# Linear attention and a bilinear feed-forward on one core: the out stage of three groups as seven block products, and v by casting transfers

## Chip, cores, metric

One core of a Trainium2 chip. The metric is device time in microseconds of one execution, from three runs; the profile is of one more execution of the same program.

## What is computed

Attention with decay in blocks, for batch 4, 8 heads, 768 positions and head size 64, and behind it a feed-forward whose two hidden halves are multiplied with each other:

```
for b in range(nb):                       # blocks of 64 positions
    intra = einsum('bhij,bhjd->bhid', einsum('bhic,bhjc->bhij', qb, kb) * Dmask, vb)
    inter = einsum('bhid,bhde->bhie', qb * lam_pow, kv_state)
    out[:, :, sl] = intra + inter
    kv_state = lam_block * kv_state + einsum('bhsd,bhse->bhde', kb * rev_pow, vb)
x = out.transpose(0, 2, 1, 3).reshape(3072, 512)
a, b = x @ w_a, x @ w_b                   # 512 -> 1536
return (a * b) @ w_out                    # 1536 -> 512, float32
```

## The kernel before

A *unit* is a block of 128 positions of one batch entry with all 8 heads: 24 units, 6 to a batch entry. The units go through the feed-forward in eight groups of 4, 1, 2, 4, 4, 4, 4 and 1 units (`GROUPS`). All matmuls are bf16, all accumulation is in the eight banks of PSUM.

**A unit's attention.** SP loads q, k and v of the unit (L154, 256 KB each in runs of 256 bytes) into staging tiles, `pump` keeping two or three units ahead. `make_ks` and `make_qs` scale k and q with powers of lambda and cast them (L318, on GpSimd from unit 6 on), `make_vb` casts v (L337 or L335, on GpSimd, VectorE or ScalarE by `VB_ENG`). From unit 7 on a DMA transpose on SP turns q and k (L346); units 4 to 6 are transposed on TensorE (L360). `piece_S` makes the scores on TensorE (L374) and masks them from PSUM on VectorE (L391); `piece_V` adds the unit to the running state (L438) and copies it (L471 on VectorE, L469 on ScalarE); `pieces_O` computes the attention of one or two units (L408), and ScalarE copies it, transposed, into the group's x tile `xT` (L431).

**A group's feed-forward.** Groups 0, 1, 2 and 7 run `ffn`: for each of 12 blocks of 128 hidden columns an a product, a ScalarE copy (L519), a b product and a VectorE multiplication into `ab` (L510, L537); then the out products, 12 matmuls of 512 columns for each unit (L557), a copy (L552 or, in the first two groups, L548) and a store. Groups 3 to 6 (`Z_GROUPS`) run `ffn_z`, in which a and b are each made by a seven-product scheme for 2 x 2 blocks: six *pairs* (index n), each of seven products of four matmuls of 256 columns (L641, `product`), three copies of partial sums on ScalarE (L647, `snap`), three subtractions on VectorE (L679, L688, L689), and `finish`: the seventh product, a ScalarE copy (L656) and the VectorE multiplication into `ab` (L658). The sums of the weights (`weight_sum`, L212 to L218) and of xT (`x_sums`, L620 to L622) that the scheme needs are VectorE's. Then comes the out stage, 48 matmuls of 512 columns for a group (L697, `out_part`), in whose midst the last pair is finished.

**What sets the order.** The program is emitted by hand: each engine executes its instructions in the order in which they are emitted, waiting on semaphores. `PLAN` lists for every group at which slot (`hook(slot)`, called between the steps of `ffn` and `ffn_z`) which piece is emitted: C casts a part of w_out, PK, PV and P prepare a unit (k and q, v, all), T transposes, S, V and O or O2 are the pieces above, Q is an O2 with two score pieces, WS is a weight sum, X the sums of xT, W stores a row that was kept back. A piece that stands at a slot only fixes the place in each engine's queue; an engine that has its inputs runs ahead of TensorE.

Of the kernel before, what the change touches and what calls it, by code (L numbers as in the profile page):

```python
# [22 lines left out]
def _bc(ap, dims):  # L23
# [8 lines left out]
W_BUFS = 8  # L32
# [10 lines left out]
PLAN = {  # L43
    0: [(0, 'V', 3), (8, 'C', 0), (9, 'C', 1), (15, 'C', 2), (18, 'C', 3), (23, 'PK', 4),
        (26, 'C', 4), (26, 'T', 4), (27, 'WS', 0), (28, 'WS', 1), (29, 'C', 5), (29, 'S', 4),
        (30, 'PV', 4), (31, 'WS', 2), (32, 'WS', 3), (33, 'O', 4), (34, 'WS', 4),
        (35, 'PK', 5), (35, 'PV', 5)],
    1: [(0, 'V', 4), (2, 'T', 5), (3, 'PK', 6), (4, 'WS', 5), (6, 'PV', 6), (6, 'S', 5),
        (7, 'T', 6), (8, 'WS', 6), (10, 'S', 6), (11, 'WS', 7), (12, 'O2', (5, 6)),
        (13, 'P', 7)],  # L50
    2: [(2, 'V', 6), (2, 'P', 8), (3, 'P', 9), (4, 'W', None), (5, 'V', 7), (5, 'PK', 10),
        (7, 'V', 8), (8, 'S', 7), (8, 'S', 8), (10, 'V', 9), (10, 'W', None), (11, 'PV', 10),
        (11, 'W', None), (12, 'P', 11), (12, 'W', None), (12, 'Q', (7, 8, 9, 10)),
        (13, 'P', 12), (14, 'O2', (9, 10)), (15, 'X', 3), (15, 'P', 13), (15, 'W', None)],
    3: [(0, 'S', 11), (2, 'P', 14), (4, 'S', 12), (7, 'S', 13), (7, 'P', 15),
        (9, 'O2', (11, 12)), (11, 'S', 14), (11, 'V', 13), (15, 'P', 16),
        (16, 'O2', (13, 14)), (16, 'X', 4), (17, 'P', 17), (17, 'P', 18), (17, 'S', 15),
        (19, 'S', 16), (19, 'P', 19)],
    4: [(3, 'V', 11), (3, 'V', 15), (4, 'S', 17), (5, 'O2', (15, 16)), (6, 'S', 18),
        (7, 'P', 20), (8, 'O2', (17, 18)), (9, 'V', 17), (9, 'P', 21), (11, 'S', 19),  # L60
        (13, 'S', 20), (14, 'X', 5), (19, 'V', 19), (19, 'P', 22)],
    5: [(4, 'S', 22), (5, 'S', 21), (8, 'O2', (19, 20)), (10, 'V', 21), (11, 'O2', (21, 22)),
        (11, 'P', 23), (16, 'X', 6)],
    6: [(0, 'S', 23), (11, 'O', 23)],
}
Z_GROUPS = (3, 4, 5, 6)
KV_ENG = dict(enumerate(["dve"] * 10 +
                        ["act"] * 2 +
                        ["dve"] +
                        ["act"] * 3 +  # L70
                        ["dve"] * 6 +
                        ["act"] +
                        ["dve"]))
VB_ENG = dict(enumerate(["pool"] * 7 +
                        ["dve"] * 3 +
                        ["act"] * 2 +
                        ["dve"] +
                        ["pool"] * 4 +
                        ["dve"] +
                        ["pool"] * 2 +  # L80
                        ["act"] +
                        ["dve"] +
                        ["pool"] * 2))
# [3 lines left out]
def kernel(  # L87
# [25 lines left out]
    wst_pool = ctx.enter_context(tc.tile_pool(name="wst", bufs=W_BUFS))  # L113
    ld_pool = ctx.enter_context(tc.tile_pool(name="ld", bufs=4))
    prep_pool = ctx.enter_context(tc.tile_pool(name="prep", bufs=6))
# [3 lines left out]
    a_pool = ctx.enter_context(tc.tile_pool(name="a", bufs=4))  # L119
# [5 lines left out]
    sum_pool = ctx.enter_context(tc.tile_pool(name="sum", bufs=1))  # L125
    ctx.enter_context(tc.manual_schedule())
# [24 lines left out]
    def load_x(w, u):  # L151
        b, nb = divmod(u, NB)
        t = ld_pool.tile([128, H, D], F32, name=w + "f", tag=w + "f")
        nc.sync.dma_start(out=t, in_={"q": qr, "k": kr, "v": vr}[w][b, nb])  # L154
        raw[u, w] = t
# [7 lines left out]
    staged = {}  # L163
    w_off = [sum(W_CHUNKS[:i]) for i in range(len(W_CHUNKS) + 1)]
# [7 lines left out]
    def load_w(kind, c):  # L172
        t = wst_pool.tile([128, 1024], F32, name="wst", tag="wst")
        if kind == "o":
            t = t[:].rearrange("p (k n) -> p k n", k=2)
# [8 lines left out]
        staged[kind, c] = t  # L184

    def cast_w(kind, c, eng):
        t = staged.pop((kind, c))
# [4 lines left out]
        if eng == "act":  # L192
            nc.scalar.copy(dst, t)
        elif eng == "first":
# [3 lines left out]
        else:  # L198
# [4 lines left out]
    wz = {kind: sum_pool.tile([128, 4, 2, HF], BF16, name="wz_" + kind, tag="wz_" + kind)  # L203
          for kind in "ab"}

    def weight_sum(i):
        kind, j = "ab"[i % 2], i // 2
        w, z = (wa_sb if kind == "a" else wb_sb), wz[kind]
        a11, a12 = w[:, 0:2, :HF], w[:, 2:4, :HF]
        a21, a22 = w[:, 0:2, HF:], w[:, 2:4, HF:]  # L210
        if j == 0:
            nc.vector.tensor_sub(z[:, 0], a22, a21)  # L212
        elif j == 1:
            nc.vector.tensor_sub(z[:, 1], a11, z[:, 0])
        elif j == 2:
            nc.vector.tensor_sub(z[:, 2], a12, z[:, 1])
        else:
            nc.vector.tensor_add(z[:, 3], a11, a21)  # L218
# [6 lines left out]
    pending += [("o", 4), ("o", 5), ("v", n0)]  # L225
    for u in range(n0 + 1, NU):
        pending += [("q", u), ("k", u), ("v", u)]
    used = {"u": 0}

    def pump():  # L230
        while pending:
            kind, c = pending[0]
            if kind in "abo":
                if len(staged) >= W_BUFS:
                    return
# [8 lines left out]
    idle_sb = singles.tile([128, 512], BF16, name="idle_sb")  # L244
# [11 lines left out]

# [368 lines left out]
    def ffn_z(g, u0, xT, hook):  # L625
# [42 lines left out]
        for n in range(NP):  # L668
            if n != 1:
                begin(n)  # L670
# [253 lines left out]
```

## Time and profile before

| | |
|---|---|
| median of three runs | 228.94 us (227.91, 228.94, 229.74) |
| profiled execution | 228.72 us |
| its span, first to last instruction | 227.0 us, TensorE clock granted 1.00 |
| q, k or v of a unit, issue to landing, median | 5.0 to 5.4 us |
| DMA transpose of a unit, issue to landing | 4.8 us |
| a stored 256 KB, issue to landing | 2.2 us |

Busy time counts the time in which an engine executes; for TensorE it is that of matmuls, which overlap, so rates are read from starts that follow each other. A row of the groups gives line, engine, operation, what it writes and reads, count, busy time and mean duration, then the idle time ahead of it and what ended that. The chain of waits goes back from the last instruction to what released each step. "SPq" is SP's own queue, in which a DMA is issued.

### The profile page before, as it was taken

What the parts mean: (1) busy time and instruction counts of PE and PEld (TensorE: products, weight loads), DVE (VectorE), ACT (ScalarE), POOL (GpSimd) and SP (SyncE); (2) the same over time, 40 slices, a digit from 0 to 9 for tenths busy, and PEclk for the clock granted to TensorE, in tenths of its full rate; (3) what the DMA queues carried; (4) which work ended last, traced back from release to release, by engine and by line L of the source; (5) the groups of instructions that cost most, each with busy time, mean ns of one, the idle gap of its engine ahead of it and who ended that gap; (6) DMA issues with size and microseconds to landing.
All of it is one profiled execution on the core that took longest, in us unless ns stands there. A gap on an engine that the chain in (4) does not pass through costs nothing.

```text
span 227.0 us, 5349 instructions
## 1 busy us (share of the span) xinstructions
PE 217.8 (96%) x2127; PEld 148.3 (65%) x2127; DVE 154.6 (68%) x257; ACT 117.0 (52%) x233; POOL 59.2 (26%) x73
## 2 busy tenths in 40 slices
PE   7798999999899999999999999999999999999994
PEld 2374444447678758877458887448887458885493
DVE  0994773969959868999356988676988318773050
ACT  2685465037443267656247685127576236672261
POOL 6061000147843254424424434460000000000000
PEclk9999999999999999999999999999999999999999
DMA  4999999999999999999999999943020030000311
GB/s 131 318 261 350 359 387 319 271 222 196 233 192 200 240 187 269 212 233 184 181 247 237 205 186 231 169 153 92 3 48 1 27 144 18 1 3 0 141 46 46
DMA packets 97544, 39.40 MB, mean 174 GB/s; under 512 B 85488, under 2 KB 92016, under 8 KB 97520
## 3 DMA queue, kind: packets, MB, share of 16 engines
q1 hardware_dynamic: 97232, 39.00, 80.4%
q8 instruction: 16, 0.26, 0.5%
q10 hardware_dynamic: 288, 0.07, 0.1%
q14 instruction: 8, 0.07, 0.1%
HBM read 28.32 MB, written 6.29 MB: 152 GB/s over the span
## 4 chain that ended last, share of the span: by engine, by line
PE 77%; DMA 8%; SPq 6%; DVE 4%; issue 2%; ACT 1%; ACTq 0%; DVEq 0%
PE op L697 18%; PE U L641 15%; PE b_ps L510 9%; PE op L557 9%; PE a_ps L510 7%; PE V L641 7%; PE o_ps L408 4%; DMA wst<-in_moe_w_b_dram 4%; PE W L641 4%; SPq L154 3%; DMA qkT<-qk 3%; PE kq L374 2%; DMA q<-in_q_dram 2%; PE kvd L438 1%; SPq L183 1%
## 5 line engine op out<-in xcount | busy, mean ns | idle before, releaser
L697 PE MATMUL op<-wo_sb,ab 128*128 128x512 bf16 x192 | 43.3, 379 | 0.0
L391 DVE TENSOR_TENSOR m<-kq,lotri 128x512 bf16<-128x512 f32 x47 | 29.7, 681 | 13.7 <-PE kq L374 13.6
L647 ACT COPY u<-U 128x512 f32<-128x512 f32 x48 | 27.8, 587 | 18.7 <-PE U L641 17.9
L318 POOL TENSOR_TENSOR qk<-kf,lp_k 128x512 bf16<-128x512 f32 x18 | 19.7, 1096 | 53.2 <-DMA kf<-in_k_dram 51.0
L537 DVE TENSOR_TENSOR ab<-a_sb,b_ps 128x128 bf16<-128x128 bf16 (+2 forms) x48 | 19.3, 415 | 20.9 <-ACT a_sb L519 13.6
L697 PEld LDWEIGHTS <-ab 128*128 128x128 bf16 x192 | 18.2, 98 | 20.7
L318 POOL TENSOR_TENSOR qk<-qf,lp_q 128x512 bf16<-128x512 f32 x20 | 24.8, 1239 | 23.0 <-DMA qf<-in_q_dram 23.0
L510 PE MATMUL b_ps<-xT,wb_sb 128*128 128x128 bf16 (+2 forms) x192 | 27.6, 272 | 1.2 <-DVE wb_sb L199 1.0
L510 PE MATMUL a_ps<-xT,wa_sb 128*128 128x128 bf16 (+2 forms) x200 | 27.7, 268 | 0.0
L552 ACT COPY o_sb<-op 128x512 f32<-128x512 f32 (+2 forms) x21 | 11.1, 547 | 31.3 <-PE op L697 28.8
L658 DVE TENSOR_TENSOR ab<-oab 128x1024 bf16<-128x1024 bf16 x24 | 18.8, 783 | 9.1 <-ACT oab L656 9.0
L519 ACT CAST a_sb<-a_ps 128x128 bf16<-128x128 f32 (+2 forms) x48 | 17.2, 376 | 13.1 <-PE a_ps L510 11.5
L557 PE MATMUL op<-wo_sb,ab 128*128 128x512 bf16 (+2 forms) x120 | 22.5, 337 | 0.2 <-DVE ab L537 0.2
L510 PEld LDWEIGHTS <-wb_sb 128*128 128x128 bf16 x192 | 15.8, 98 | 7.7 <-DVE wb_sb L199 1.5
L641 PEld LDWEIGHTS <-wz_a 128*128 128x128 bf16 x192 | 18.3, 98 | 3.3 <-issue 0.3
L510 PEld LDWEIGHTS <-wa_sb 128*128 128x128 bf16 x200 | 16.0, 98 | 6.7 <-DVE wa_sb L199 0.4
L641 PEld LDWEIGHTS <-wz_b 128*128 128x128 bf16 x192 | 18.7, 97 | 2.2
L688 DVE TENSOR_TENSOR oab<-U,v 128x512 bf16<-128x512 f32 x24 | 16.4, 683 | 3.4 <-PE U L641 2.6
L641 PE MATMUL U<-xT,wz_a 128*128 128x256 bf16 x96 | 18.3, 272 | 0.0
L641 PE MATMUL U<-xT,wz_b 128*128 128x256 bf16 x96 | 18.3, 272 | 0.0
L679 DVE TENSOR_TENSOR oab<-W,u 128x512 bf16<-128x512 f32 x24 | 16.3, 681 | 0.9 <-PE W L641 0.9
L431 ACT CAST xT<-o_ps 128x512 bf16<-128x512 f32 (+1 forms) x24 | 12.2, 556 | 9.0 <-PE o_ps L408 8.9
(96 smaller groups left out, 337.0 us busy)
## 6 DMA issues: line engine op xcount, KB each, us to landing
vf<-in_v_dram SPq DMA_DIRECT2D x24, 256.0 KB, 5.0
qf<-in_q_dram SPq DMA_DIRECT2D x20, 256.0 KB, 5.1
kf<-in_k_dram SPq DMA_DIRECT2D x20, 256.0 KB, 5.4
out_dram<-o_sb SPq DMA_DIRECT2D x18, 256.0 KB, 2.2
wst<-in_moe_w_a_dram SPq DMA_DIRECT2D x6, 512.0 KB, 8.4
wst<-in_moe_w_b_dram SPq DMA_DIRECT2D x6, 512.0 KB, 9.0
wst<-in_moe_w_out_dram SPq DMA_DIRECT2D x6, 512.0 KB, 9.1
out_dram<-o_kept SPq DMA_DIRECT2D x5, 256.0 KB, 4.6
```

What stands on the lines that cost most here:

```text
L318: eng_of(eng).tensor_mul(dst.rearrange("p (c b) d -> p b c d", b=2), x[:].rearrange("p (b c) d -> p b c d", b=2), lp.rearrange("p (b c) o ...
L391: nc.vector.tensor_mul(m, kq[i], lotri_bc)
L510: nc.tensor.matmul(ps[:, lo:hi], lhsT=w_sb[:, s, f * 128:(f + 1) * 128], rhs=xT[:, s, lo:hi], start=(s == 0), stop=(s == KS - 1), skip_gro ...
L519: nc.scalar.copy(a_sb[:, :gt], ps[:, :gt])
L537: nc.vector.tensor_mul(ab[:, f, :gt], a_sb[:, :gt], ps[:, :gt])
L557: nc.tensor.matmul(op[:, lo:hi], lhsT=ab[:, f, t * 128:(t + 1) * 128], rhs=wo_sb[:, f, lo:hi], start=(f == 0), stop=(f == FC - 1))
L641: nc.tensor.matmul(ps[:, k, :], lhsT=wt[:, s, n * 128:(n + 1) * 128], rhs=rhs[i][:, s, :], start=(fresh and k == 0 and s == 0), stop=True, ...
L647: nc.scalar.copy(t, ps)
L658: nc.vector.tensor_mul(ab[:].rearrange("p (h i) (t c) -> p h i t c", h=2, t=2)[:, :, n], o5[:, :, :, 0, :], o5[:, :, :, 1, :])
L679: nc.vector.tensor_sub(oab[:, 2], W, d["u1"])
L688: nc.vector.tensor_sub(oab[:, 1], d["U"], v1)
L697: nc.tensor.matmul(ops[t][:].rearrange("p a b -> p (a b)"), lhsT=ab[:, f, t * 128:(t + 1) * 128], rhs=wo_sb[:, f, :], start=(f == 0), stop ...
```

## The change

It was described as: out stage of three 4-unit groups as seven block products between the next group's pairs, v of later units by casting transfers, no sums on GpSimd. In the code:

- The out stage of groups 4, 5 and 6 (`ZO_GROUPS`) becomes a seven-product scheme too: seven products of 12 matmuls of 256 columns, each cut into two halves (`out_half`, piece H), emitted at slots of the next group, between the products of its pairs (or the steps of group 7). It needs sums of blocks of `ab` (`ab_sum`, piece SM, eight half sums a group) and of w_out (`out_sum`, piece WO, five, once). Three partial sums a group are copied by ScalarE, three results subtracted by VectorE, one copied by ScalarE; four stores a group as before.
- `ffn_z` has three slots a pair in place of two. With halves of an earlier group in its plan (`joined`), X and W share bank 2 and the last product of a pair comes after the next pair's first one; banks 3 and 4 are the out stage's.
- v of units 4 to 23 is loaded by a DMA that GpSimd issues and that casts to bf16 on the way (`prep_v`). `VB_ENG` is left for units 0 to 3.
- Which engine does what is in new tables: 2 of the weight sums, 2 of the five w_out sums, 5 of the sums of xT and 10 of the 24 half sums of `ab` are GpSimd's; 5 of 6 casts of w_out go to ScalarE; eight masks are copied from PSUM by ScalarE first (`MASK_ACT`); some state copies change engine.
- Staging of the weights uses tiles that are free early on, in place of a pool of its own; other pools are renamed or resized. `PLAN` is new throughout.

```diff
 PLAN = {
...
+    1: [(1, 'PK', 6), (1, 'WS', 5), (2, 'PV', 6), (3, 'PV', 5), (4, 'T', 5), (5, 'T', 6),
+        (7, 'S', 6), (8, 'P', 7), (10, 'S', 5), (13, 'WS', 6), (13, 'O2', (5, 6)),
+        (13, 'P', 8), (13, 'WS', 7), (13, 'P', 9)],
+    2: [(1, 'S', 7), (1, 'V', 6), (1, 'W', None), (4, 'PK', 10), (4, 'S', 8), (5, 'V', 7),
...
+    4: [(1, 'P', 19), (1, 'S', 17), (1, 'V', 15), (4, 'O2', (15, 16)), (5, 'S', 18),
+        (10, 'O2', (17, 18)), (10, 'SM', (4, 0)), (12, 'S', 19), (14, 'P', 20), (14, 'X', 5),
+        (17, 'SM', (4, 2)), (17, 'SM', (4, 4)), (17, 'P', 21), (17, 'P', 22)],
+    5: [(0, 'S', 20), (1, 'SM', (4, 1)), (1, 'H', (4, 0)), (1, 'SM', (4, 3)), (1, 'V', 19),
+        (2, 'H', (4, 1)), (2, 'O2', (19, 20)), (4, 'H', (4, 2)), (5, 'S', 21), (5, 'P', 23),
+        (5, 'H', (4, 3)), (5, 'SM', (4, 5)), (6, 'V', 21), (6, 'S', 22), (7, 'H', (4, 4)),
...
+    7: [(0, 'H', (6, 0)), (0, 'SM', (6, 1)), (0, 'H', (6, 1)), (0, 'SM', (6, 3)),
+        (0, 'H', (6, 2)), (0, 'SM', (6, 5)), (1, 'H', (6, 3)), (4, 'H', (6, 4)),
...
+ZO_GROUPS = (4, 5, 6)
+FIN_AT = 5
+N_LATE = 3
...
     def prep_v(u):
-        make_vb(u, VB_ENG[u])
+        vb = vb_pool.tile([128, H, D], BF16, name="vb", tag="vb")
+        b, nb = divmod(u, NB)
+        nc.gpsimd.dma_start(out=vb, in_=vr[b, nb])
+        U[u]["vb"] = vb
         pump()
...
         for n in range(NP):
+            oab = oab_pool.tile([128, 4, 2, 256], BF16, name="oab", tag="oab")
+            U = z_bank("U", pairs[0] % 2)
+            pairs[0] += 1
+            product(U, n, 1, True)
+            u1 = snap(U)
+            if joined:
+                if fin:
+                    fin.pop()()
+                hook(3 * n)
+            X = z_bank("V", 2 if joined else 2 + n % 2)
+            product(X, n, 4, True)
+            v1 = snap(X)
+            if not joined:
+                hook(3 * n)
+                W = z_bank("W", 4)
+                product(W, n, 0, True)
+                nc.vector.tensor_sub(oab[:, 2], W, u1)
+            product(U, n, 5)
+            u2 = snap(U)
+            if not joined and fin:
+                fin.pop()()
+            hook(3 * n + 1)
+            product(X, n, 6)
+            if joined:
+                nc.vector.tensor_sub(oab[:, 3], X, u2)
+            product(U, n, 3)
+            nc.vector.tensor_sub(oab[:, 1], U, v1)
+            if not joined:
+                nc.vector.tensor_sub(oab[:, 3], X, u2)
+            hook(3 * n + 2)
+            if joined:
+                W = z_bank("W", 2)
+                product(W, n, 0, True)
+                nc.vector.tensor_sub(oab[:, 2], W, u1)
+            fin.append(lambda n=n, U=U, oab=oab: last_product(n, U, oab))
...
+    def ab_sum(g, i):
...
+        eng = eng_of(SUM_ENG[g, i])
+        if j == 0:
+            eng.tensor_add(z3, a11, a21)
+        elif j == 1:
+            eng.tensor_sub(a21, a22, a21)
+        elif j == 2:
+            eng.tensor_sub(z1, a11, a21)
+        else:
+            eng.tensor_sub(z1, a12, z1)
+
+    O_ORDER = (4, 1, 5, 6, 3, 0, 2)
+
+    def out_half(g, i):
+        d = outs[g]
+        p, h = O_ORDER[i // 2], i % 2
...
+        for n in range(h * NP // 2, (h + 1) * NP // 2):
+            for t in range(2):
+                nc.tensor.matmul(ps[:, t, :], lhsT=lhs[p][:, n, t * 128:(t + 1) * 128],
+                                 rhs=rhs[:, n, :], start=fresh, stop=True, skip_group_check=True)
+                fresh = False
+        if h:
+            if p in (4, 1, 5):
+                d[{4: "v1", 1: "u1", 5: "u2"}[p]] = snap(ps)
+            else:
+                o = o_pool.tile([128, 2, 256], F32, name="o_sb", tag="osb")
+                if p == 2:
+                    nc.scalar.copy(o, ps)
+                else:
+                    nc.vector.tensor_sub(o, ps, d[{6: "u2", 3: "v1", 0: "u1"}[p]])
...
+                nc.sync.dma_start(out=rows.rearrange("t p n -> p t n"), in_=o)
```

## The prediction

> **What bounds the kernel now.** I read the page first: engines' busy time, the slices, the chain. Then the busy time by stage, then PE's instructions in order of time, and last the queues of GpSimd (POOL) and SP.
>
> ```profile
> PE 217.8 (96%) x2127; PEld 148.3 (65%) x2127; DVE 154.6 (68%) x257; ACT 117.0 (52%) x233; POOL 59.2 (26%) x73
> ...
> PE   7798999999899999999999999999999999999994
> ...
> POOL 6061000147843254424424434460000000000000
> PEclk9999999999999999999999999999999999999999
> DMA  4999999999999999999999999943020030000311
> ...
> PE 77%; DMA 8%; SPq 6%; DVE 4%; issue 2%; ACT 1%; ACTq 0%; DVEq 0%
> ```
>
> TensorE is busy in all slices but the first few and the last, at the full granted clock, and holds 77% of the chain: the kernel is PE-bound. DMA is full until about 145 us. POOL is done at 151 us.
>
> ```profile
> 52.20:65.20 13.00, 11.62 (x171) 8.82 (x169) 11.28 (x23) 6.46 (x18) 10.60 (x9) 1.00 1.12 200
> ...
> 119.30:153.10 33.80, 33.55 (x327) 23.74 (x326) 27.21 (x40) 18.36 (x36) 15.85 (x16) 1.00 1.11 198
> 153.10:186.40 33.30, 33.30 (x334) 24.08 (x331) 20.84 (x34) 18.95 (x37) 0.00 (x0) 1.00 0.18 49
> 186.40:216.00 29.60, 29.47 (x241) 21.20 (x236) 16.30 (x26) 15.13 (x30) 0.00 (x0) 1.00 0.10 37
> ```
>
> These are stages (length; PE, weight load, DVE, ACT, POOL busy; clock; DMA): group 1, and groups 4, 5 and 6, each with its out stage. In groups 4 to 6 PE is never free, DVE has 7 to 13 us over. Only group 1 has PE short: there DVE is 87% busy and POOL 82%.
>
> ```profile
> 200.58 0.88 PE U L641 x8
> 205.87 9.73 PE op L697 x45
> ```
>
> Two lines of the chain of waits: a 256-column matmul costs 0.88 / 8 = 0.110 us, a 512-column one 9.73 / 45 = 0.216. Every one has its own weight load in both. So half the columns cost half the time here.
>
> ```profile
> 53.66 0.39 PE L360 MATMUL tps<-ident,qk 128*128 128x128 bf16 x4
> 54.54 0.40 PE L360 MATMUL tps<-ident,qk 128*128 128x128 bf16 x4 [0.49 <-DVE qk L318]
> ...
> 57.30 0.39 PE L510 MATMUL b_ps<-xT,wb_sb 128*128 128x128 bf16 x4
> 58.30 0.61 PE L360 MATMUL tps<-ident,qk 128*128 128x128 bf16 x8 [0.61 <-DVE ab L537]
> ```
>
> PE in group 1: four such matmuls follow each other in 0.22 us, so the two marked waits cost 0.88 - 0.22 = 0.66 and 1.00 - 0.22 = 0.78 us. Two smaller ones (59.70 and 61.56 us) cost 0.29 and 0.32: 2.05 us in all, behind DVE's casts, weight sums and the scaling of k.
>
> **The change part by part.** The sum goes against the profiled execution: 228.72 us, span 227.0 and 1.7 around it; the median shown is 228.94, 0.2 above it.
>
> 1. *Out products.* Per group 48 matmuls of 512 columns become 7 x 12 = 84 of 256: 48 x 0.216 = 10.37 us become 84 x 0.110 = 9.20. Saved 1.17, three groups: **-3.5 us**, all on the path since PE is. The same matmul form stands in the trace 672 times (L641), so I see little room: -3.2 to -3.8.
>
> 2. *DVE.* Added: 9 subtractions from PSUM (L688: 0.683) = 6.1; 14 half sums of 768 elements, half of the 0.945 for 1536 (L212) = 6.6; 3 sums of wo = 2.8. Removed: 6 casts of v (0.70), 5 of wo (0.78), 2 weight sums, 5 sums of xT, 2 state copies, and 8 masks get a bf16 source: about 17. Net -1.5 us. In groups 5 and 6 the out stage no longer gives DVE its 10 us of rest, but the same work is spread over the same length: 6 x (3 x 0.60 + 0.7) = 15 for the pairs (starts are 0.60 apart in a run), 5 masks, 2 out, 3 sums: 25 of 33 us. Throughput costs nothing; order can (rival 2).
>
> 3. *ACT.* 8 raw copies (0.59), 5 casts of wo (1.045), 4 half state copies (0.37) more, 3 casts of v (0.62) less: +9.5 us on 117. The casts of wo run beside the out stage of group 0, where ACT was busy 15.5 of 34 us. Nothing.
>
> 4. *Group 1.* DVE loses there 4 casts of wo, a weight sum and the late scaling of k of unit 5 (moved from slot 35 of group 0 to 29). Of the 2.05 us I take 1.5 as gained; the two transposes are now a slot apart and the scores of unit 6 two slots later, behind two ACT copies of 1.01 us (L362), which leaves about 0.5. **-1.5**, bounds -2.05 and 0.
>
> 5. *Other waits of PE* in groups 3 to 7 (98.2, 139.5, 142.2, 196.0, 216.3 us) sum to 1.5 us by the same reading. The last pair's finish is moved from after 3 to after 5 out matmuls (FIN_AT), or into the next group's first pair: **-1.0**, bounds -1.5 and 0.
>
> 6. *v by casting transfers.* SP loses 20 issues of 0.7 to 2.1 us, so q and k come earlier by about a quarter. POOL loses 11 casts (0.68 = 7.5 us) and gets 20 issues, of a price D that the trace does not show: it has no DMA issued by POOL. Below: 0.57, SP's issue of a q load that waits for nothing. Above: if POOL wrote two entries for each of the 1024 runs of 256 B at its own rate per element (L389: 1155 ns / 512 = 2.26 ns), 4.6 us. I take 1.1, since SP's issue of the very same transfer (0.7 to 1.3 in most rows) is nearest. The deadlines: v of units 6 and 5 are issued ahead of k and q of unit 7, v of 7 ahead of unit 8. POOL: qf of unit 5 at 46.7, a weight sum of 3 us, k and q of unit 6 until 52.6 us, two D, two scalings (2.34 by the L318 means), transfer 5.7 (the chain has 5.74): scores of unit 7 can start at 60.6 + 2D, PE asks at about 65; of unit 8 at 63 + 3D, asked at 69. So D up to about 2 is hidden, and over it each us costs three. v of unit 5 lands at 52.6 + 2D + 5 and is asked at 62. At 1.1: 0.
>
> 7. *Sums on POOL.* The short description says no sums on GpSimd; the instruction order of the changed kernel has 19 there (2 weight, 2 wo, 5 of xT, 10 of ab), 17,920 elements in all: at 1155 ns for 512, 40 us more. POOL: 59 - 7.5 + 40 + 22 = 114 us of 227, so enough in sum. The due ones: from the last evacuation of units 17 and 18, POOL does z_add 2.3, z_mix 1.2, a half sum 1.7, units 21 and 22 (2.34 + D each), two half sums: 1.5 + 13.3 + 2D = 17.0 until the half sum (4,3), which product half 3 of group 5 needs 18.1 us after (5.1 of pairs, 13 of halves, scores and finish). Next (4,5): 22.2 against 23. Third, z_sub, z_add, z_mix for group 6: 1.5 + 5.8 = 7.3 against 7.1. Margins of +1, +0.8, -0.2; with POOL's 1.04 us scalings reaching 1.81 beside DVE I take **+1.5**, bounds 0 and 6.
>
> ```profile
> 59.40 1.04 POOL L318 TENSOR_TENSOR qk<-kf,lp_k 128x512 bf16<-128x512 f32 x1 [0.45 <-DMA kf<-in_k_dram]
> 60.40 1.81 POOL L318 TENSOR_TENSOR qk<-qf,lp_q 128x512 bf16<-128x512 f32 x1
> ...
> 115.96 0.69 DVE L621 TENSOR_TENSOR z_add<-xT 128x1024 bf16<-128x1024 bf16 x1
> 149.29 1.52 DVE L621 TENSOR_TENSOR z_add<-xT 128x1024 bf16<-128x1024 bf16 x1
> ```
>
> These rows show what the two engines do to each other: the same operation 1.04 and 1.81 us on POOL, 0.69 and 1.52 on DVE, the slow one each time with the other at work.
>
> 8. *Group 7.* The halves of group 6 now lie between the 12 short a and b steps. The second half product needs the last ab, which is there after finish 0.44, ACT 0.59, DVE 0.7: 1.7 us, PE gets there after 1.1. **+0.6**, and 0.2 for subtractions that queue. Bounds 0 and 2. The tail behind the last matmul (3 us) stays; the four stores of group 6 land by then (2.2 us each).
>
> 9. *New waits between pairs* (bank 2 for both X and W): in all 12 pairs a half product, a score or an out piece lies between the subtraction that frees the bank and the product that needs it, 0.66 against 0.6 + 0.1. **+0.5**, bounds 0 and 4.
>
> Sum: -3.5 - 1.5 - 1.0 + 0 + 1.5 + 0.8 + 0.5 = -3.2: 228.72 - 3.2 = **225.5 us**.
>
> A rule that speaks against part 6: the Trainium skill (SBUF — State Buffer, "SBUF: two separate sides") says that VectorE operations in a two-port mode, such as tensor_copy, keep GpSimd from writing its descriptors, and gives 620 ns for such a DMA alone and 3100 ns beside one. At D = 3.1 my part 6 would be 3 x 1.1 = 3.3 and the estimate 228.8. No run here shows it yet; DVE's last cast comes ahead of all v but that of unit 4, and the same page expects no such effect of two-input operations.
>
> **Rivals.**
> *POOL late (slower).* One mechanism: D. Scores of unit 8 wait for k behind three issues, so the time is 225.5 + 3 (D - 2). It is over the time before by 1% from D = 3.9; at 4.6 it is 233, and then POOL's 60 us of other work plus 20 D would also pass the 133 us between v of unit 4 and unit 23 (20 us over: 245 at worst). For it: POOL was 82% busy in group 1 and its issues stand in the one queue. Against: SP makes the same transfer in about 1 us. **0.18**, at 234.
>
> *Waits eat the gain (no change).* Parts 7 and 9 at the upper bounds: sums on POOL 1.75 times as long (1.81 / 1.04) make the half sums 3 us and z_mix 3 us late, or bank 2 costs 0.35 in each of 12 pairs = 4.1. For it: margins under 1 us, and DVE at 1.52 where POOL works. Against: POOL runs ahead of PE elsewhere. 225.5 + 3 = 228.5. **0.24**.
>
> *More is gained.* Parts 4 and 5 at full, nothing of 7 to 9: 228.7 - 7 = 221.7. **0.04** for under 222.8. That the change does not do what it says holds for the sums alone and is in the sum.
>
> **How the numbers follow.** Likeliest 225.5, by itself 223 to 226.6, 0.54 (and the 0.04 beyond). About 1% is what a measurement here can tell from no change: 226.65 to 231.2. Faster 0.58, same 0.24, slower 0.18. The range leaves out 0.04 below and most of the 0.18: 222.8 to 231.2.
>
> **What would show it.** Right: 252 matmuls of 256 columns in groups 5 to 7 at 0.110 each; group 1 shorter by 1.5 us; POOL's DMA rows near 1.1 us; PE without waits over 0.5 us in group 2. Wrong: PE waiting for qkT in group 2 (part 6), for zab, ab or z_mix on POOL in groups 5 and 6 (part 7), or for oab in every pair (part 9).

## The result, and the profile after

The changed kernel takes 247.58 us (four runs, 247.01 to 250.45), the kernel before beside it 228.99 us (227.91 to 229.74): 1.084 times as long, interval 1.074 to 1.094. The forecast was 225.5 us, with a range up to 231.2. The profiled execution of the changed kernel took 247.01 us, its span is 245.3; against the profiled execution before that is 18.3 us more. (In the ratios below, runs over 1.5% above the fastest of the same kernel are left out, so that a ratio can lie under that of the medians.)

The page of the changed kernel, the lines that answer to those shown of before:

```profile
PE 221.0 (90%) x2225; PEld 162.6 (66%) x2235; DVE 177.4 (72%) x263; ACT 125.8 (51%) x247; POOL 107.6 (44%) x101
...
PE   7889999957999999899991999669999999999994
...
POOL 5060006799806306364997505959040931320000
PEclk9999999988999999999997699979999999999999
...
PE 69%; DVE 13%; DMA 6%; issue 5%; ACT 3%; SPq 2%; ACTq 0%; DVEq 0%
```

TensorE, which was busy in all slices, now has holes in slices 9 and 10, 22, and 26 and 27, in all of which POOL is at work for half of the time or more, and the granted clock falls in or behind each. VectorE holds 13% of the chain, not 4%, and is busy 177.4 us, not 154.6.

What TensorE waited for in the changed kernel (total, times, longest):

```profile
PE kq L445 <- DVE m L468: 5.7, 2, 5.4
PE U L718 <- DVE oab L757: 5.2, 4, 3.5
PE o_ps L485 <- DVE m L468: 2.5, 1, 2.5
PE b_ps L584 <- DVE ab L611: 1.7, 1, 1.7
...
PE b_ps L584 <- ACT oab L724: 0.5, 1, 0.5
```

Four of the five rows end with VectorE: 15.1 us. The stretches in which the granted clock was halved, with the columns of the stage rows in the prediction (length; PE, weight load, DVE, ACT, POOL busy; clock; DMA):

```profile
53.60:57.00 3.40, 3.40 (x23) 2.32 (x22) 2.03 (x2) 2.10 (x5) 3.39 (x5) 0.50 1.54 195
132.10:138.90 6.80, 4.68 (x29) 3.35 (x29) 6.10 (x8) 1.86 (x4) 4.30 (x5) 0.50 0.99 174
162.80:166.20 3.40, 3.40 (x21) 2.54 (x19) 2.66 (x3) 2.14 (x5) 2.57 (x2) 0.50 1.52 192
```

TensorE was busy 11.48 us of these 13.6 at clock 0.50. Two of its 256-column matmuls take 0.43 us there (starts at 136.67 and 137.10) and 0.22 at the full clock, so half of the 11.48, 5.7 us, is lost (an estimate). 15.1 + 5.7 = 20.8 us against the 18.3 to be explained; what the change saves stands on the other side.

The longest wait, first VectorE, then GpSimd in the same stretch:

```profile
123.57 1.27 DVE L468 TENSOR_TENSOR m<-kq,lotri 128x512 bf16<-128x512 f32 x2
124.77 8.46 DVE L275 TENSOR_TENSOR wy<-wo_sb 128x1536 bf16<-128x1536 bf16 x1
133.15 1.27 DVE L468 TENSOR_TENSOR m<-kq,lotri 128x512 bf16<-128x512 f32 x2
```

```profile
124.28 6.14 POOL L275 TENSOR_TENSOR wy<-wo_sb 128x1536 bf16<-128x1536 bf16 x2
130.37 1.03 POOL L386 TENSOR_TENSOR qk<-kf,lp_k 128x512 bf16<-128x512 f32 x1
131.37 1.03 POOL L386 TENSOR_TENSOR qk<-qf,lp_q 128x512 bf16<-128x512 f32 x1
132.36 0.95 POOL L422 DMA_DIRECT2D vb<-in_v_dram  x1
```

A sum of w_out on VectorE, 0.95 us by the like sums, takes 8.46. It ends at 133.23, so by its usual length it did its work from about 132.3 us on, when GpSimd's second scaling ended and only a DMA issue followed. Until then it was *held*. Behind it in VectorE's queue stands the mask that TensorE waits for (5.39 us). The same is seen at a scaling of k (3.57 us at 47.59) and two weight sums (2.56 and 2.69). Masks and subtractions with one input in PSUM keep their 0.68 us everywhere.

Most holds are shorter. Of the 18 operations of VectorE in this kernel that took over 0.3 us longer than by themselves, 14 waited for one operation of GpSimd only, also where GpSimd's next one followed at once. Here a sum of w_out on VectorE got in between two scalings, and the second scaling took 1.75 us in place of 1.03:

```profile
116.65 1.50 DVE L275 TENSOR_TENSOR wy<-wo_sb 128x1536 bf16<-128x1536 bf16 x1
```

```profile
117.30 1.75 POOL L386 TENSOR_TENSOR qk<-qf,lp_q 128x512 bf16<-128x512 f32 x1
```

The other four, the 8.46 us among them, waited over two to four operations.

The scheme itself is there: the matmuls of the half products start 0.109 us apart in the chain (1.97 us for 18), and a DMA issue costs GpSimd 0.94 us:

```profile
225.33 1.97 PE op L840 x18
```

```profile
L422 POOL DMA_DIRECT2D vb<-in_v_dram x20 | 18.8, 942 | 0.0
```

### The profile page after: what moved, and what is told of

Its sections match the earlier page's. It is cut to its first block, busy times and chain, and to the rows that moved or that the text cites. A ratio compares the mean times of both kernels' runs of the same rounds, so it can differ in the third digit from the quotient of the medians.

```text
span 245.3 us, 5567 instructions
## 1 busy us (share of the span) xinstructions
PE 221.0 (90%) x2225; PEld 162.6 (66%) x2235; DVE 177.4 (72%) x263; ACT 125.8 (51%) x247; POOL 107.6 (44%) x101
## 4 chain that ended last, share of the span: by engine, by line
PE 69%; DVE 13%; DMA 6%; issue 5%; ACT 3%; SPq 2%; ACTq 0%; DVEq 0%
PE U L718 15%; PE op L840 12%; PE a_ps L584 8%; PE b_ps L584 8%; PE V L718 8%; PE op L631 5%; PE W L718 4%; PE o_ps L485 3%; DVE ab L726 3%; DMA wst<-in_moe_w_a_dram 2%; PE kq L445 2%; SPq L178 2%; DMA q<-in_q_dram 2%; DMA qf<-in_q_dram 2%; DVE m L468 2%
## 5 line engine op out<-in xcount | busy, mean ns | idle before, releaser
L386 POOL TENSOR_TENSOR qk<-kf,lp_k 128x512 bf16<-128x512 f32 x18 | 20.3, 1130 | 33.8 <-DMA kf<-in_k_dram 17.9
L726 DVE TENSOR_TENSOR ab<-oab 128x1024 bf16<-128x1024 bf16 x24 | 22.6, 940 | 12.6 <-ACT oab L724 12.4
L584 PE MATMUL a_ps<-xT,wa_sb 128*128 128x128 bf16 (+2 forms) x199 | 28.3, 272 | 1.2 <-ACT xT L508 0.5
L468 DVE TENSOR_TENSOR m<-kq,lotri 128x512 bf16<-128x512 f32 x39 | 24.9, 680 | 1.0 <-PE kq L445 0.9
L386 POOL TENSOR_TENSOR qk<-qf,lp_q 128x512 bf16<-128x512 f32 x20 | 23.3, 1166 | 1.4 <-DMA qf<-in_q_dram 1.4
L584 PEld LDWEIGHTS <-wa_sb 128*128 128x128 bf16 x200 | 16.9, 100 | 8.1 <-issue 1.6
L718 PEld LDWEIGHTS <-wa_sb 128*128 128x128 bf16 x144 | 13.7, 99 | 8.8 <-issue 6.1
L422 POOL DMA_DIRECT2D vb<-in_v_dram x20 | 18.8, 942 | 0.0
L724 ACT CAST oab<-U 128x512 bf16<-128x512 f32 x24 | 14.2, 591 | 7.1 <-PE U L718 7.1
L757 DVE TENSOR_TENSOR oab<-U,u 128x512 bf16<-128x512 f32 x24 | 16.4, 681 | 1.5 <-PE U L718 1.4
L631 PEld LDWEIGHTS <-ab 128*128 128x128 bf16 x120 | 10.3, 99 | 8.0
```

What stands on the lines that cost most here:

```text
L386: eng_of(eng).tensor_mul(dst.rearrange("p (c b) d -> p b c d", b=2), x[:].rearrange("p (b c) d -> p b c d", b=2), lp.rearrange("p (b c) o ...
L422: nc.gpsimd.dma_start(out=vb, in_=vr[b, nb])
L468: nc.vector.tensor_mul(m, kq[i], lotri_bc)
L584: nc.tensor.matmul(ps[:, lo:hi], lhsT=w_sb[:, s, f * 128:(f + 1) * 128], rhs=xT[:, s, lo:hi], start=(s == 0), stop=(s == KS - 1), skip_gro ...
L631: nc.tensor.matmul(op[:, lo:hi], lhsT=ab[:, f, t * 128:(t + 1) * 128], rhs=wo_sb[:, f, lo:hi], start=(f == 0), stop=(f == FC - 1))
L718: nc.tensor.matmul(ps[:, k, :], lhsT=wt[:, s, n * 128:(n + 1) * 128], rhs=rhs[i][:, s, :], start=(fresh and k == 0 and s == 0), stop=True, ...
```

## Experiments

*Theory A.* While GpSimd executes operations that read two tensors in SBUF, VectorE's operations with two SBUF inputs stand still; what is queued behind them comes late, TensorE waits, and its granted clock halves (0.50 in the rows above). *Rival B*: the joined pairs and the new order of pieces make TensorE wait, whoever does the sums. *Rival C*: the casting transfers do it. Medians with their ranges, and ratios:

| kernel | us | ratio to before |
|---|---|---|
| all 19 sums on VectorE | 241.7 (237.0 to 242.9) | not given |
| w_out sums on VectorE | 236.9 (233.4 to 240.2) | 1.026 [1.021, 1.032] |
| weight sums on VectorE | 245.1 (241.4 to 246.2) | 1.065 [1.056, 1.073] |
| both of these on VectorE | 238.4 (237.1 to 239.0) | 1.041 [1.032, 1.051] |
| memset behind each operation | 245.0 (242.4 to 245.9) | 1.068 [1.058, 1.077] |
| w_out sums on VectorE, GpSimd writes | 238.8 (237.1 to 240.0) | 1.042 [1.032, 1.051] |
| the same, GpSimd copies | 240.7 (238.7 to 244.0) | 1.052 [1.046, 1.057] |
| all sums on VectorE, v loaded | 239.9 (239.3 to 241.2) | 1.052 [1.048, 1.056] |
| before, v by casting transfers | 234.2 (233.9 to 238.7) | 1.022 [1.013, 1.030] |
| sums of xT for group 5 late | 233.2 (230.6 to 233.6) | 1.019 [1.014, 1.025] |
| weight sums placed as well (*sums placed*) | 229.4 (228.9 to 230.0) | 1.005 [1.003, 1.007] |
| sums placed, v loaded | 232.8 (231.2 to 237.4) | 1.018 [1.011, 1.025] |
| sums placed, one-input scalings | 287.4 (285.7 to 289.3) | 1.258 [1.252, 1.263] |
| before, one-input scalings | 265.3 (264.7 to 266.9) | 1.162 [1.157, 1.167] |
| changed, one-input scalings | 298.8 (298.7 to 299.3) | 1.307 [1.303, 1.312] |
| sums placed, masks from PSUM | 229.0 (227.9 to 231.5) | 1.004 [1.002, 1.005] |
| that, xT sums inside the pair | 233.2 (231.0 to 234.1) | 1.021 [1.016, 1.025] |

### Which sums cost the time

```diff
-WS_ENG = {0: 'pool', ..., 3: 'pool', ...}     # third run
-WO_ENG = {..., 2: 'pool', ..., 4: 'pool'}     # second run
+all 'dve'; in the first run SUM_ENG and XS_ENG too
```

> All 19 sums that GpSimd has in the changed kernel (2 weight sums, 2 sums of w_out, 5 of xT, 10 half sums of ab) go to VectorE; plan and everything else stay. Theory A (a sum on GpSimd that reads SBUF keeps VectorE's operations with two SBUF inputs waiting, TensorE then waits for masks and subtractions, and the granted clock halves behind each long wait): the pauses at 51.8, 61.4, 133.9 and 161.5 us (2.7 + 1.9 + 5.6 + 3.7 us) and the 13.6 us at clock 0.5 go for the most part, 247 - 14 - 6 = 227 us, 224 to 232, although VectorE has 19 operations more. Rival B (the joined pairs, bank 2 for two tiles and the new order of pieces make TensorE wait, whoever does the sums): over 242 us, for VectorE's queue only gets longer. Rival C (the casting transfers that GpSimd issues are what holds VectorE up): over 240 us, as they stay.

> Of the changed kernel only the two w_out sums on GpSimd go to VectorE. Theory A: the sum on VectorE that took 8.46 us takes 0.95, the pause of 5.6 us at 133.9 and the 6.8 us at clock 0.5 behind it go: 5.6 + 0.5 x 6.8 = 9 us, 238 us (235.5 to 240.5). Rivals B and C: 246 to 248, the pause stays.

> Of the changed kernel only the two weight sums on GpSimd go to VectorE. Theory A: the scaling of k of 3.57 us at 47.6 us and the weight sums of 2.6 us beside the other one fall to their own 0.95 to 1.1 us; the pauses of 2.7 and 1.9 us and half of 3.4 us at clock 0.5 go: 6 us less, 241 us (238.5 to 244). If GpSimd's scalings of q and k, which stay, hold VectorE up just as well: 244 to 247. Rivals B and C: 246 to 248.

The second came as A had it, 9 us less by its expectation: 10.7 us less by the medians, 13 by the ratios (1.084 to 1.026). VectorE in that run:

```profile
124.53 1.81 DVE L275 TENSOR_TENSOR wy<-wo_sb 128x1536 bf16<-128x1536 bf16 x2
127.68 0.95 DVE L275 TENSOR_TENSOR wy<-wo_sb 128x1536 bf16<-128x1536 bf16 x1
```

Three sums in 2.8 us in place of one in 8.46, and no wait of TensorE over 0.4 us between 120 and 147 us. C falls as the cause of that wait, since the casting transfers stayed. The first and the third missed A's numbers. With the weight sums on VectorE the wait at 51.8 us was gone, but one of 3.4 us stood at 57.4: a weight sum now waited for GpSimd's scalings. With all sums on VectorE new waits came from 140 us on (2.8, 2.1, 1.2, 1.1 us; these waits, those of the run with copies and those of part 9 below are read from the starts of the matmuls, up to 0.17 us more than the idle time in brackets), behind sums of xT and half sums that VectorE itself had not got to; about 1.1 us of the first are a hold by GpSimd's scalings (z_sub 0.92 us, z_add 1.52). So A is right for the hold and too simple for the time: VectorE, busy 169 us of 235, has little room in a queue that TensorE needs in order. B has a share, too: the wait of 1.2 us, at 184.7, is for bank 2, which the subtraction of W frees late behind three sums of xT.

### What it is that holds VectorE

```diff
+            nc.gpsimd.memset(nop, 0.0)      # 128 x 16, behind each scaling, weight, w_out and half sum on GpSimd
```

> The changed kernel with one memset of 128 x 16 elements on GpSimd behind each of its sums and each of its scalings of q and k; nothing else moves. The memset reads nothing. If the lock is held for one instruction at a time and VectorE only loses the race for it when two instructions of GpSimd stand back to back, the w_out sum on VectorE of 8.46 us becomes 3.5 to 5 us, the pause of 5.6 us shrinks to 1 to 2, and the whole is 4 to 8 us shorter: 240 to 243 us. If GpSimd keeps VectorE out until it runs out of work, whatever the work, the sum stays near 8.4 us and the time near 247.5.

```profile
121.45 7.75 DVE L276 TENSOR_TENSOR wy<-wo_sb 128x1536 bf16<-128x1536 bf16 x1
```

```profile
122.18 3.11 POOL L276 TENSOR_TENSOR wy<-wo_sb 128x1536 bf16<-128x1536 bf16 x1
125.22 0.12 POOL L387 MEMSET nop<- 128x16 bf16 x1
125.28 3.09 POOL L276 TENSOR_TENSOR wy<-wo_sb 128x1536 bf16<-128x1536 bf16 x1
128.31 0.12 POOL L387 MEMSET nop<- 128x16 bf16 x1
128.46 1.63 POOL L393 TENSOR_TENSOR qk<-kf,lp_k 128x512 bf16<-128x512 f32 x1
```

Neither expectation fits. VectorE was let in at about 128.3 us (7.75 - 0.95 after its start), at the second memset, not at the first, and then GpSimd's scaling was the one that waited (1.63 us). A gap between two operations can end the hold but need not, and it can end without a gap (116.65 us above). VectorE's sum had also come 0.7 us before GpSimd's first one, while GpSimd was still issuing a transfer. What decides stays open.

```diff
-        eng = gpsimd for two w_out sums
+        eng = vector; beside it on GpSimd, for each: 6 x memset(nop)                    # first run
+                                               or 6 x tensor_copy(nop, wo_sb[:, f, :])  # second run
```

> The two w_out sums go from GpSimd to VectorE as in the run at 236.9 us, and in the place of each GpSimd gets six memsets of 128 x 512 (0.48 us each by the rows of the prologue, 2.9 us for one sum of 3.07). GpSimd is as late with what follows, but reads nothing. Theory A (it is the reading beside VectorE's two inputs): the sums on VectorE take 0.95 us each, within 2 us of 236.9: 235 to 239. Rival (GpSimd's queue is late with q, k and v of the units behind, or any work of GpSimd holds VectorE up): a pause of 4 us or more near 132 us and 243 us or more.

> As the run with twelve memsets on GpSimd (238.8 us), with twelve copies of 128 x 512 bf16 from w_out in their place: GpSimd reads one input. If any read of SBUF by GpSimd holds VectorE's operations with two SBUF inputs up, the w_out sums on VectorE that lie beside them take 3 us or more and the time is 242 to 248 us; if it takes two inputs on GpSimd's side too, they take 0.95 and the time is 236 to 240.

The memsets took GpSimd 6.95 us (12 of 128x512), more than the two sums (6.14). VectorE's sums beside them took 0.95 us or less each, and no wait stood near 132 us. So the cause is not that GpSimd is late, nor any work of GpSimd. With the copies, GpSimd first:

```profile
122.56 10.54 POOL L277 COPY nop<-wo_sb 128x512 bf16<-128x512 bf16 x12
```

```profile
123.08 2.22 DVE L278 TENSOR_TENSOR wy<-wo_sb 128x1536 bf16<-128x1536 bf16 x2
126.43 0.94 DVE L278 TENSOR_TENSOR wy<-wo_sb 128x1536 bf16<-128x1536 bf16 x1
```

Ten microseconds of GpSimd reading one tensor cost three sums on VectorE 0.4 us in all (one of them took 1.36). The median, 240.7, is 0.7 above the range expected, but its waits (2.7 us at 51.6, 3.7 at 153.2, 1.6 at 139.3) are those of the other places.

### The casting transfers

```diff
-        make_vb(u, VB_ENG[u])                  # kernel before; the other way round in the other two
+        nc.gpsimd.dma_start(out=vb, in_=vr[b, nb])
```

> The kernel before with one part of the change alone: v of units 4 to 23 by casting transfers that GpSimd issues, with no casts of v on any engine; the loads of q and k then follow each other on SP. The prediction's part 6 (0, with GpSimd 7.5 us of casts less and 18.8 us of issues more): 227 to 230 us. Rival C (the transfers hold something up): 233 us or more. If the casts taken from VectorE and GpSimd are worth something in group 1: 225 to 227.

> All sums on VectorE as in the run before, and beside it v of units 4 to 23 loaded by SP in float32 and cast on GpSimd, VectorE and ScalarE as in the kernel before the change (the load tiles of v are shared with those of q and k). Theory A: the casting transfers themselves cost about nothing, GpSimd gets 11 casts of 0.7 us and loses 20 issues of 0.94 us: within 2 us of all sums on VectorE, 225 to 231, slower if at all. Rival C (casting transfers hold VectorE or the queues up): at least 4 us faster than all sums on VectorE.

> From the run with the sums placed: v loaded by SP and cast on the engines as before the change. q and k come later, so GpSimd's scalings lie further apart, with casts of v between them. If the denser scalings are what the casting transfers cost (part 6 alone cost 5 us on the kernel before), the time falls by 1 to 4 us; if the sums were placed out of their way, nothing is left of that, and SP's 20 more loads cost 0 to 3 us.

On the kernel before, this part alone costs 5.3 us by the medians (234.15 against 228.85), 4.9 by the ratio. VectorE, GpSimd and TensorE there:

```profile
56.37 4.38 DVE L216 TENSOR_TENSOR wz_b<-wb_sb,wz_b 128x1536 bf16<-128x1536 bf16 x1
```

```profile
57.09 1.06 POOL L318 TENSOR_TENSOR qk<-kf,lp_k 128x512 bf16<-128x512 f32 x1
58.09 1.04 POOL L318 TENSOR_TENSOR qk<-qf,lp_q 128x512 bf16<-128x512 f32 x1
59.08 0.94 POOL L354 DMA_DIRECT2D vb<-in_v_dram  x1
60.04 1.62 POOL L318 TENSOR_TENSOR qk<-kf,lp_k 128x512 bf16<-128x512 f32 x1
```

```profile
61.01 0.38 PE L363 MATMUL tps<-ident,qk 128*128 128x128 bf16 x4 [3.53 <-DVE ab L540]
```

It is the same hold, with no sum on GpSimd: q and k arrive earlier, GpSimd scales four units one behind the other, and a weight sum on VectorE lands among them. The row is longer than the two scalings that it spans and its own 0.95 us together; a DMA issue lies at both ends, and whether it has a part in the hold is not shown. (At 103 us ScalarE waits 2.92 us for a stored row to leave. I put that down to SP's changed order of issues in this kernel; it was not tested.) With sums placed (below), loading v is 3.5 us *slower* by the medians than the casting transfers, 2.8 by the ratios; with all sums on VectorE, the medians are 1.8 us apart with overlapping ranges. So C does not explain the loss of the changed kernel: what the transfers cost depends on what VectorE has in its queue when GpSimd's scalings come.

### Sums where nothing stands behind them

The first run has the weight and the w_out sums on VectorE. The second starts from the first and the third from the second; these two also make z_mix ahead of z_add in every group.

```diff
 0: [... (31, 'O', 4),
-    (34, 'V', 4), (35, 'WS', 3), (35, 'WS', 4)],
+    (31, 'WS', 3), (31, 'WS', 4), (34, 'V', 4)],            # third run
-1: [(1, 'PK', 6), (1, 'WS', 5), ..., (13, 'WS', 6),
+1: [(1, 'PK', 6), ..., (13, 'WS', 5), (13, 'WS', 6),        # third run
-4: [..., (14, 'X', 5),
+4: [..., (17, 'X', 5),                                      # second and third run, all on VectorE
```

> Of the changed kernel the two weight sums and the two w_out sums on GpSimd go to VectorE; the late sums (5 of xT, 10 half sums of ab) stay on GpSimd. Theory A, as mended (the lock is real, but where VectorE has no slack, from 140 us on, its own queue is too long for all sums, so the late sums are better on GpSimd): with the w_out sums moved 236.9 was measured, the two pauses in groups 0 and 1 left there (2.7 + 1.7 us, and 1.7 for the clock behind them) go: 231 us, 229 to 234. Rival (moving sums only moves the pause, as the run with the weight sums alone, 245.1 instead of the 241 expected, suggests): 235 us or more.

> From the run with weight and w_out sums on VectorE (238.4 us): the sums of xT for group 5 all go to VectorE and move from slot 14 of group 4 (behind the fifth pair) to slot 17 (behind the last), z_mix ahead of z_add. GpSimd no longer has 3.4 us of them ahead of a half sum and two scalings. Theory A: the multiplications of 1.90 and 2.44 us and the pause of 3.7 us at 151 us, with half of 3.4 us at clock 0.5 behind it, go; z_sub makes TensorE wait about 0.7 us at the start of group 5 instead: 238.4 - 3.7 - 1.7 + 0.7 = 233.7 us, 232 to 236. Rival (the bank that the last product of a pair shares with the next pair is what makes TensorE wait there, whatever VectorE does): 237 to 240.

> From the run just named, three weight sums move on VectorE as well: two from behind the last slot of group 0 to slot 31, where VectorE had nothing for 2 us, one from the first slot of group 1 to its out stage, where TensorE asks nothing of VectorE. GpSimd's work stays as it is. Theory A: a weight sum may still wait for GpSimd's scalings, but no multiplication of group 1 stands behind it; the pause of 3.4 us at 57.4 and half of 3.4 us at clock 0.5 go: 233.7 - 3.4 - 1.7 = 228.6 us, 226.5 to 231. Rival (GpSimd's scalings hold VectorE's next operation, whichever it is): under 2 us less than the run before it.

The first missed (238.4, 231 expected): its rival was right, the wait only moved, to 57.4 us. The other two came within 0.8 us of A's numbers: 233.2 (233.7) and 229.4 (228.6). VectorE with the weight sums placed:

```profile
49.53 0.95 DVE L256 TENSOR_TENSOR wz_b<-wb_sb,wz_b 128x1536 bf16<-128x1536 bf16 x1
50.40 1.80 DVE L258 TENSOR_TENSOR wz_a<-wa_sb,wz_a 128x1536 bf16<-128x1536 bf16 x1
52.12 0.68 DVE L548 TENSOR_TENSOR st<-kvd,bdiag 128x512 bf16<-128x512 f32 x1
...
60.79 1.87 DVE L258 TENSOR_TENSOR wz_b<-wb_sb,wz_b 128x1536 bf16<-128x1536 bf16 x1
```

Weight sums are still held (1.80, 1.87 in place of 0.95), but nobody waits behind them, no wait of TensorE behind the first 18 us reaches 1.1 us, and the granted clock is 0.998 over the span. So 18.2 of the 18.6 us are taken back, by the medians, with the scheme, the casting transfers and 13 sums on GpSimd left in place.

### What is left

```diff
+        if eng == "pool":                     # each of q and k, per head
+            nc.gpsimd.tensor_scalar_mul(dst[:, 2 * c + b, :], x[:, h, :], lp[:, h, :])
```

> From the run with the sums placed (229.4 us): GpSimd's scalings of q and k, one operation with two SBUF inputs of 512 columns (1.03 us), become eight of 64 columns each, which multiply by one value per partition and so read one tensor. Twelve copies with one input did not hold VectorE up. Theory A: what VectorE still loses to GpSimd (167.4 us busy, about 10 more than its operations take by themselves) goes for the most part, VectorE 160 us or less, and half of the 6.5 us of small pauses of TensorE: 226.5 us, 224.5 to 228.5. Rival (the rest lies in the new plan: the banks and VectorE's and ScalarE's queues between the pairs): 228.5 to 231. If eight small operations cost GpSimd over 2 us, it is late and the time over 231.

> The same edit on the kernel before the change, whose only operations with two SBUF inputs on GpSimd are these scalings. Theory A: VectorE's 154.6 us fall by 4 or more, but TensorE hardly waited for it: 226.5 to 228.5 us. Rival (GpSimd gets late by the smaller operations): 230 or more.

> The same edit on the changed kernel, whose sums on GpSimd keep their two inputs. Theory A: the w_out sum on VectorE that took 8.46 us still waits for the two w_out sums on GpSimd, but not for the two scalings behind them: about 6.5 us; the scaling of k at 47.6 us still waits for the weight sum beside it; the multiplications of 1.90 and 2.44 us near 155 us fall to 0.7 to 1.5. 240 us, 236 to 243. If the sums alone were the cause: 246 to 248. If the scalings alone were: 232 or less.

GpSimd's groups in the first, then VectorE's:

```profile
L389 POOL TENSOR_SCALAR qk<-qf,lp_q 128x64 bf16<-128x64 f32 x160 | 77.3, 501 | 22.6 <-DMA qf<-in_q_dram 22.5
```

```profile
L731 DVE TENSOR_TENSOR ab<-oab 128x1024 bf16<-128x1024 bf16 x24 | 17.6, 735 | 15.9 <-ACT oab L729 15.8
L275 DVE TENSOR_TENSOR wy<-wo_sb 128x1536 bf16<-128x1536 bf16 x5 | 4.7, 948 | 0.0
```

As a cure it fails on all three kernels: an operation of 64 columns costs 0.50 us, eight of them 4 us for a scaling of 1.03, and GpSimd becomes the bound. But the rows on VectorE are what A asks for: with GpSimd at work 192 us, the w_out sums take 0.948 us and VectorE is busy 160.8 us. On the kernel before it is 149.4, 5.2 us less than without the edit, so that kernel held VectorE up too, where nobody waited.

The third run's time separates nothing for the same reason, but its trace does. Each run has 304 of the small scalings on GpSimd. In the third only two operations of VectorE were over 0.3 us late (7.66 and 4.96 us), each behind GpSimd's two-input sums, and let in when the scalings came. VectorE and GpSimd at the first, a mask with two SBUF inputs, 0.42 us by itself:

```profile
169.86 7.66 DVE L465 TENSOR_TENSOR m<-raw_kq,lotri 128x512 bf16<-128x512 bf16 x1
```

```profile
171.09 6.13 POOL L275 TENSOR_TENSOR wy<-wo_sb 128x1536 bf16<-128x1536 bf16 x2
177.20 1.87 POOL L389 TENSOR_SCALAR qk<-kf,lp_k 128x64 bf16<-128x64 f32 x4
```

The mask ends at 177.52, so it was let in at about 177.1, as the two sums ended. (It had come 1.2 us before them, while GpSimd was issuing a transfer, like the sum in the run with memsets.) In the changed kernel the two-input scalings behind these sums had to pass as well. One-input operations are not wholly free: on the kernel before, a weight sum took 1.67 us and a multiplication 1.08 beside the small scalings.

```diff
+MASK_ACT = dict.fromkeys(range(24), 0)                     # both runs
-(17, 'X', 5)
+(15, 'X', 5)                                               # second run
```

> From the run with the sums placed (229.4 us): no mask is copied from PSUM by ScalarE first; all are made from PSUM, with one SBUF input. The eight masks with two SBUF inputs took 0.72 us each on VectorE there (up to 1.48 beside GpSimd, 0.41 by themselves); from PSUM one costs 0.60 and never waits for GpSimd, and ScalarE has 4.7 us less. Theory A: 0.5 to 1.5 us less, 228 to 229. Rival (the rest is the order between the pairs): 229 to 230.

> As the run before it, and the sums of xT for group 5 stand at slot 15 of group 4, in the midst of the last pair, in place of behind it. The waits of 0.84 and 0.27 us at the start of group 5 were for VectorE's subtraction and for z_sub. If GpSimd's lock is what made the old place cost 3.7 us, the sums take 1.8 us here and the waits move into the last pair: within 0.7 us of the run before it, either way. If VectorE has no slack inside a pair: 1 to 2 us slower.

Masks from PSUM give 229.0, inside both expectations, so the run does not tell them apart. The second run was 4.2 us slower than it, more than either branch had. VectorE and TensorE there:

```profile
142.48 1.85 DVE L684 TENSOR_TENSOR z_sub<-xT 128x1024 bf16<-128x1024 bf16 x1
```

```profile
147.12 0.38 PE L709 MATMUL U<-z_sub,wa_sb 128*128 128x256 bf16 x2 [2.97 <-DVE oab L748]
```

Only 1.2 us of that wait is the hold (1.85 against 0.68); the rest is the work of three sums in the midst of a pair. In the changed kernel, where GpSimd had two of the three, VectorE's operations at that place (two multiplications of 1.90 and 2.44 us, z_sub of 1.33, each 0.69 by itself) were held for 3.6 us, as long as the wait of 3.5. Giving the sums to VectorE there exchanges the hold for the work itself. So B is right in this: inside a pair VectorE has room for neither. In the kernel before these sums lay beside the out stage (slot 14, with slots 0 to 11 in the pairs). None of these versions beats the kernel before.

## Why the prediction was wrong

The stretch from the end of group 4's pairs to the end holds all products that the scheme changes. Before, and with sums placed and masks from PSUM:

```profile
141.22:227.00 85.78, 82.22 (x756) 58.14 (x752) 48.97 (x83) 40.53 (x84) 6.11 (x6) 1.00 0.25 61
```

```profile
141.50:226.20 84.70, 79.00 (x861) 68.89 (x859) 57.31 (x97) 41.96 (x90) 24.51 (x17) 1.00 0.35 60
```

1. *Out products, -3.5*: right. TensorE is busy 3.2 us less (82.22 to 79.00), at 0.109 us a matmul. The stretch is shorter by 1.1 only: the rest went into waits (9).
2. *DVE, -1.5, "throughput costs nothing; order can"*: this is where it failed. VectorE came to 177.4 us, not 153.1. With one-input scalings it is busy 160.8 us; less the 4.9 us of sums that the changed kernel has on GpSimd that is 155.9, against 149.4 for the kernel before with the same edit. So its own work grew by some 6 us in place of falling by 1.5. In part that is because the casts taken away were priced with their waits (v at 0.70 us, 0.42 by itself) and the half sums at 0.47 (0.55 measured). The other 21.5 us are operations held by GpSimd, against 5.2 before. The new operations were priced as if VectorE were alone.
3. *ACT, nothing*: right, 125.8 us (126.5 by the sum) and no long wait for it.
4. *Group 1, -1.5*: 14.2 us in the changed kernel (55.6 to 69.8) against 13.0 before, so +1.2. With its sums placed it takes 11.9 us (52.0 to 63.9 in the run with masks from PSUM): -1.1. The gain was there, and the hold and the halved clock behind it ate it.
5. *Other waits, -1.0*: not found. Group 3 takes 35.2 us in that same run, 34.2 before.
6. *Casting transfers, 0 at D = 1.1*: D is 0.94 and GpSimd was not late. The 3100 ns that the Trainium skill gives (SBUF — State Buffer, "SBUF: two separate sides") did not occur. But the term left out what earlier q and k do: by itself +5.3 us, part of it in the same hold.
7. *Sums on POOL, +1.5 (0 to 6)*: the other half of the failure. I asked when GpSimd's sums would be ready, and took the rows 1.04 against 1.81 and 0.69 against 1.52 as two engines slowing each other by a factor. They are waits: one stands still for one of the other's operations, or several. By the medians the two w_out sums cost 10.7 us, the sums for group 5, with their place, 5.2, and the weight sums 2.3 (the time rose by 1.5 when only their engine was changed and fell by 3.8 with the place). By the ratios it is 13.2, 5.1 and nothing (up 3.4, down 3.2). The Trainium skill has this waiting (SBUF — State Buffer, "Who interferes with whom"): a VectorE instruction with two SBUF inputs contends with a GpSimd instruction that reads SBUF, and the loser blocks for the whole instruction. I cited that page for its other rule. The trace agrees on the blocking (8.46 us for 0.95), and differs twice: twelve copies with one input cost 0.4 us in all, and this hold went through two sums and two scalings, not one instruction.
8. *Group 7, +0.8*: right; TensorE waits 0.5 us there for ScalarE's last copy of group 6.
9. *Waits between pairs, +0.5 (0 to 4)*: too small, in the main by VectorE's and ScalarE's queues. In the 84.7 us above I read waits of 1.07, 0.45, 0.30 and 0.83 us, 2.6 in all. The 0.83 us, at 177.6, are bank 2 as the term had it: the subtraction of W comes late behind a half sum held for 1.68 us.

The clock was in no term: 5.7 us that follow from the waits. With the sums placed and the masks from PSUM, the last stretch is 1.1 us shorter and group 1 as well, and groups 2 and 3, 0.5 and 1.0 us longer, take most of that back: -0.7. The two profiled executions differ by -0.8 us (227.92 and 228.72), the medians by +0.9 (229.0 and 228.1). So without the long holds the scheme gains nothing that these runs can tell, where -3.2 was forecast. Of the rivals, "waits eat the gain" had the nearest mechanism, priced at a sixth of what it cost, and "POOL late" the right side for a reason that did not occur.

## What to carry to other kernels

Before an elementwise operation is given to GpSimd, list what VectorE executes at that time with both inputs in SBUF, and its casts from SBUF. Price each at the length of one of GpSimd's two-input operations, and at worst at that of GpSimd's whole run of them. Operations of VectorE that read PSUM were never held here, memsets on GpSimd held nothing, and its one-input copies next to nothing. Then look at what stands behind it in VectorE's queue: a held sum costs nothing where TensorE asks for nothing (18 us came back by giving nine operations another engine or place), and 10 us where a mask follows. Busy time summed from rows of one engine alone does not show this; a VectorE or GpSimd row of 1.5 times its usual length, with the other at work, was a wait here and not a rate.

## What the runs showed of the hardware that was not expected

- A hold can last over GpSimd operations that follow each other: two sums and two scalings, 7.5 us, and a memset of 0.12 us between them ended it once and once not. In 14 of 18 cases in the changed kernel it lasted for one operation.
- A cast on VectorE, with one input in SBUF, is held too: in the kernel before, a cast of v took 1.25 us at 82.94 us, beside a scaling of q on GpSimd, in place of 0.42.
- TensorE's granted clock fell to 0.50 for 3.4 us or a multiple of that (6.8 above) in or behind waits of 1.4 us (sums placed and v loaded, at 151 us) and more, but not after one of about 2 us (all sums on VectorE, at 172 us) nor one of 2.97 (xT sums inside the pair). It matters where a wait lies, and not only its length. The three drops of the changed kernel begin 78.5 and 30.7 us apart, 23 and 9 times 3.41. In the 3.41 us ahead of them TensorE was busy 1.55, 0.00 and 1.35 us; in the 3.41 us before that last stretch, with the start of the same wait, 1.91, and the clock stayed. The Trainium skill (TensorE: Matmul & The Clock Gate, "What's actually happening") gives windows of 3.4 us that run freely and half rate after an idle one. The length agrees, but the windows ahead of two of the three drops were not idle.
- A GpSimd operation of 64 columns with one value per partition costs 0.50 us, half of what two full inputs of 512 columns cost (1.03).
